# Hyena filter and maxout FFN: the filter's second stage by halves, with one sum moved to GpSimd

## The chip, the cores and the metric

The kernel runs on one core of one Trainium2 chip. The metric is the device time in microseconds (us) of one execution; for the kernel before it is the median of three runs. One further execution was recorded by the hardware profiler, and every line of a profile below is from it. The engines are named as in the profile: PE is TensorE's matmul, PEld its weight load, DVE is VectorE, ACT is ScalarE, POOL is GpSimd, SP is SyncE (which issues DMAs).

## The reference

The first block is a long convolution by FFT, gated by x; the second is a feed-forward block with the maximum of three products. Shapes: x and v are 4 x 12544 x 128, the filter's features 64, the FFN's width 768.

```python
def _attn_ref(x, v, pos_emb, w1, w2) -> np.ndarray:
    B, S, D = x.shape
    h_mlp = np.maximum(pos_emb @ w1, 0.0) @ w2
    pos = np.arange(S, dtype=np.float32)
    window = np.exp(-0.01 * pos)[:, None]
    h_filt = h_mlp * window
    u = x * v
    L = 2 * S
    Uf = np.fft.rfft(u, n=L, axis=1)
    Hf = np.fft.rfft(h_filt, n=L, axis=0)
    y = np.fft.irfft(Uf * Hf[None, :, :], n=L, axis=1)[:, :S, :]
    return (x * y).astype(np.float32)

def _moe_ref(x, w1, w2, w3, w_out) -> np.ndarray:
    h = np.maximum(np.maximum(x @ w1, x @ w2), x @ w3)
    return (h @ w_out).astype(np.float32)
```

## The kernel before

The transforms are matmuls with tables, in two stages each way. A sequence position is split into a block number and a place s2 in the block (0 to 127). The first stage transforms over the block numbers and leaves 90 frequencies, each a complex number (two 64-row halves of 128 partitions) for each place s2. The second stage goes over the places, with one 128 x 256 table per frequency (`wt_const`) that also holds the twiddle factors. The places are kept in two sets of 64 (r = 0 and 1: odd and even places, in reversed order), so a frequency's second stage is two matmuls, one for each r, and the outputs of a frequency and of its partner half a turn on are the sum and the difference of the two.

The prologue loads the weights, computes the filter's small MLP, and leaves two tiles of first-stage spectra: `spec` of u = x * v for batch 0 (128 partitions x 90 frequencies x 2 halves r x 128 channels) and `specH` of the filter's 64 features (128 x 90 x 2 x 64). The filter's second matmul, `w2`, is applied after the transform.

Then comes the first loop, which is where the change lies. It runs over 45 groups g of two neighbouring frequencies (k = 0, 1), one group entering at each step s, with the work of several groups in flight:

- `s_minus(g)` (L1103, POOL) stores the negated r = 0 half of the group's columns of specH in `minus`.
- `s_second(g)` (L1115, PE; L1120, ACT) is the filter's second stage. For each k, r and q it multiplies a 128 x 64 piece of specH by a 128 x 128 table into the upper or lower 64 partitions (q) of one PSUM bank: q = 0 adds both halves r, q = 1 adds the r = 1 half to the negated r = 0 half. ACT copies the 128 x 256 result to `G`.
- `g_second(g)` (L167 through `second` and `halves_mm`; ACT copies the even half to `eo`, L203) is the same stage for the signal, with 8 matmuls, and `g_butterfly(g)` (L197 and L198, DVE) makes its sum and difference, from PSUM and `eo`, in `xt`.
- One step later `g_swap` (L623, L624, ACT) writes `xs`, the real and imaginary halves of xt exchanged, one of them negated; `s_filter` (L1133, PE) applies `w2x` to G, 16 matmuls of 64 x 64 tiles, and ACT copies the 128 x 1024 product to `ht` (L1149).
- Two steps later `s_store` (L1154, POOL) stores ht in `hd`, in DRAM, for the other batches. The pointwise product of signal and filter is `g_re` (L629: xt times the filter's real part), `g_im` (L633: xs times its imaginary part, L634: the sum of both), and `g_unfold` (L641) makes sum and difference of the partners in `ab`.
- Three steps later `g_third` (L167 on `ab`, PE) is the first inverse stage; ACT copies it to `zs` (L656) and SP stores that in `zd`.

Engines run their instructions in the order in which the program issues them; semaphores are set between engines where tiles are handed on. Within a step the order of the calls is: s_second(s), s_minus(s+1), g_second(s), g_swap(s-1), s_filter(s-1), g_third(s-3), s_store(s-2), then for the group s-2 g_re, g_im and g_unfold, then g_butterfly(s). In the later steps the first units of batch 1 are loaded, multiplied (`u_mul`, L386 on DVE, in five steps of the loop) and transposed (`u_turn`, L399 and L402, in four). Steps 45 to 47 drain the loop and mix in more of batch 1.

Buffers that matter: `G`, `xt`, `xs`, `ab` and the filter's PSUM bank have two, `ht` two for even groups and two more (in the `uT` pool) for odd groups below 34; from group 34 on two in all. The PSUM banks of g_second and g_third are a pool of three.

From about 300 us to the end run the fused loops: inverse transform and FFN of batch b interleaved with the convolution of batch b + 1, and a last batch with a seven-product scheme. Nothing of it is changed. Three rows of it serve as measures: L596, L599 and L603 are its product, sum on POOL, and unfold, of the same sizes as L633, L634 and L641.

Of the kernel before, what the change touches and what calls it, by code (L numbers as in the profile page):

```python
# [10 lines left out]
FP32 = mybir.dt.float32  # L11
I32 = mybir.dt.int32
U16 = mybir.dt.uint16
ALU = mybir.AluOpType
ACTF = mybir.ActivationFunctionType
PSUM = bass.MemoryType.PSUM
P = 128
# [78 lines left out]
def kernel(  # L96
# [15 lines left out]
    nc = tc.nc  # L112
    NG, _, _, B, NB = x.shape
    FO, S = posT.shape
    D = w2.shape[1]
    DFF = moe_w1.shape[1]
    NF = DFF // P
    NK = N1 // 2
# [76 lines left out]
    def butterfly(ps, eo, xs):  # L195
        v = ps[:, :].rearrange("p (k r d) -> p k r d", k=2, r=2)
        nc.vector.tensor_tensor(out=xs[:, :, 0, :], in0=eo[:], in1=v[:, :, 0, :], op=ALU.add)  # L197
        nc.vector.tensor_tensor(out=xs[:, :, 1, :], in0=eo[:], in1=v[:, :, 0, :],  # L198
                                op=ALU.subtract)
# [80 lines left out]
    specH = pin.tile([P, N1, 2, FO], FP32, name="specH")  # L280
# [6 lines left out]
    w2x = pin.tile([P, D], FP32, name="w2x")  # L287
# [96 lines left out]
    def u_mul(u, eng=nc.vector):  # L384
        a, v = us[u]
        eng.tensor_tensor(out=a[:], in0=a[:], in1=v[:], op=ALU.mult)  # L386
# [221 lines left out]
    def g_second(g):  # L608
        ps = state["cv"][1].tile([P, 512], FP32, tag="cv", name="ps2")
        second(ps, ws.pop((g, 0)), g)  # L610
        eo = state["cv"][0].tile([P, 2, D], FP32, tag="eo", name="eo", bufs=2)
        evens(ps, eo)
        pss[g], eos[g] = ps, eo

    def g_butterfly(g):
        xt = state["cv"][0].tile([P, 2, 2, D], FP32, tag="x", name="xt", bufs=state["xb"])
        butterfly(pss.pop(g), eos.pop(g), xt)
        xts[g] = xt

    def g_swap(g):  # L620
        xt = xts[g]
        xs = state["cv"][0].tile([P, 2, 2, D], FP32, tag="xs", name="xs", bufs=2)
        nc.scalar.mul(xs[0:64], xt[64:128], -1.0)  # L623
        nc.scalar.copy(xs[64:128], xt[0:64])  # L624
        xss[g] = xs

    def g_re(g):
        xt = xts[g]
        nc.vector.tensor_tensor(out=xt[:], in0=xt[:], in1=hts[g][0][:], op=ALU.mult)  # L629

    def g_im(g, apart=False):
        xt, xs = xts[g], xss.pop(g)
        nc.vector.tensor_tensor(out=xs[:], in0=xs[:], in1=hts.pop(g)[1][:], op=ALU.mult)  # L633
        (nc.gpsimd if apart else nc.vector).tensor_tensor(  # L634
            out=xt[:], in0=xt[:], in1=xs[:], op=ALU.add)
# [9 lines left out]
    def g_third(g):  # L645
        w, ab = ws.pop((g, 1)), abs_.pop(g)
        ps = state["cv"][1].tile([P, 512], FP32, tag="cv", name="ps3")
        for k in range(2):
            for q in range(2):
                halves_mm(ps[:, (2 * k + q) * D:(2 * k + q + 1) * D], w[:, k, q, :],  # L650
                          ab[:, k, q, :], k == 0 and q == 0, True)
        if g < NK - 2:
            zs = state["cv"][0].tile([P, 2, 256], FP32, tag="z", name="zs", bufs=2)
        else:
            zs = lwp.tile([P, 2, 256], FP32, tag="w1", name="zs")
        nc.scalar.copy(zs[:].rearrange("p k f -> p (k f)"), ps[:])  # L656
        nc.sync.dma_start(
            zd[0][2 * g:2 * g + 2].rearrange("k c t f -> (c t) k f"), zs[:])
# [309 lines left out]
    def load_dir(g, a):  # L968
        w = lwp.tile([P, 2, 2, P], FP32, tag=f"w{a}", name="wt")
        nc.sync.dma_start(w[:].rearrange("p k r m -> p (k r m)"), wt_d[g, :, a, :])  # L970
        return w
# [60 lines left out]
    for f in range(0, FO, 4):  # L1032
        quad([hs[:, f + i] for i in range(4)], (f1h[:, 0], f1h[:, 1]), specH[:, :, :, f:f + 4])
        u, k = divmod(f // 4, 4)
# [10 lines left out]
    wf, wi = {}, {}  # L1045
    for u in range(4, NU, 2):
        t = uts.pop(u)
        for v in range(2):
            if u + 4 < NU:
                u_mul(u + 4 + v)  # L1050
            at = 4 * (u + v)
# [17 lines left out]
    for i in (1, 2):  # L1069
        nc.vector.tensor_tensor(out=w_sb[i][:], in0=w_sb[i][:], in1=w_sb[0][:],  # L1070
                                op=ALU.subtract)
# [3 lines left out]
    cvp = pro.enter_context(tc.tile_pool(name="cvp0", bufs=3))  # L1075
# [10 lines left out]
    def bank():  # L1086
        return next(free)

    state = {"cv": (cvp, cps), "xb": 2, "bank": bank, "wide": ("ht", 2),
             "turn": lambda: sps.tile([P, 512], FP32, tag="pl", name="pst")}  # L1090
    Gs, minus = {}, {}

    def fold(f):
        pt = cps.tile([P, 512], FP32, tag="cv", name="pt")
# [2 lines left out]
        nc.scalar.copy(w1t[:, 0], pt[:, 0:D])  # L1097
        return lambda: halves_mm(pl[:, 0:D], w1t[:, 0], wo_sb[:, f, :], f == 0, f == NF - 1)

    def s_minus(g):  # L1100

        m = cvp.tile([P, 2, FO], FP32, tag="minus", name="minus", bufs=1)
        nc.gpsimd.tensor_single_scalar(m[:], specH[:, 2 * g:2 * g + 2, 0], -1.0, op=ALU.mult)  # L1103
        minus[g] = m

    def s_second(g):


        ps = gps.tile([P, 512], FP32, tag="g", name="gps")
        m = minus.pop(g)  # L1110
        for k in range(2):
            for r in range(2):
                for q in range(2):
                    lhsT = m[:, k] if q and r == 0 else specH[:, 2 * g + k, r, :]
                    nc.tensor.matmul(ps[64 * q:64 * q + 64, k * P:(k + 1) * P],  # L1115
                                     lhsT, wf[g][:, k, r, :],
                                     start=(k == 0 and r == 0), stop=True,
                                     skip_group_check=True)
        G = cvp.tile([P, 2, 2, 64], FP32, tag="G", name="G", bufs=2)
        nc.scalar.copy(G[:].rearrange("p k c j -> p (k c j)"), ps[:, 0:2 * P])  # L1120
        Gs[g] = G

    def s_filter(g):


        G = Gs.pop(g)
        ps = sps.tile([P, 1024], FP32, tag="h", name="sps")
        for ri in range(2):
            for k in range(2):
                for q in range(2):  # L1130
                    for h in range(2):
                        at = 512 * q + (2 * ri + k) * D
                        nc.tensor.matmul(  # L1133
                            ps[64 * h:64 * h + 64, at:at + D],
                            G[64 * q:64 * q + 64, k, ri, :], w2x[64 * q:64 * q + 64],
                            start=(ri == 0 and k == 0), stop=True, skip_group_check=True)
        v = ps[:].rearrange("p (q m d) -> p m q d", q=2, d=D)
        if g == NK - 1:
            hts[g] = []
            for c in range(2):  # L1140
                ht = lwp.tile([P, 2, 2, D], FP32, tag="w0", name="ht")
                nc.scalar.copy(ht[:], v[:, 2 * c:2 * c + 2])
                hts[g].append(ht)
            return
        if g % 2 and g < NK - 11:
            ht = utp.tile([P, 2, 2, 2, D], FP32, tag="uT", name="ht")
        else:
            ht = cvp.tile([P, 2, 2, 2, D], FP32, tag="ht", name="ht", bufs=2)
        nc.scalar.copy(ht[:].rearrange("p r k q d -> p (r k) q d"), v)  # L1149
        hts[g] = ht[:, 0], ht[:, 1]  # L1150

    def s_store(g):
        for c in range(2):
            nc.gpsimd.dma_start(  # L1154
                hd[g, 64 * c:64 * c + 64],
                hts[g][c][64 * c:64 * c + 64].rearrange("p k q d -> p (k q d)"))
# [7 lines left out]
    def folding(f):  # L1164
        folded.append(fold(f))
        if len(folded) > 2:
            folded.pop(0)()

    def unit(u):
        u_first(u, (bank(), bank()), "x")  # L1170

    s_minus(0)
    for s in range(NK + 3):
        if s < NK:
            ws[s, 0] = wf[s]
            s_second(s)
            if s + 1 < NK:
                s_minus(s + 1)
            g_second(s)
            wf.pop(s)  # L1180
            if s + 3 < NK:
                wf[s + 3] = load_dir(s + 3, 0)
        if 1 <= s <= NK:
            g_swap(s - 1)
            s_filter(s - 1)
        if s >= 3:
            ws[s - 3, 1] = wi.pop(s - 3)
            g_third(s - 3)
            if s < NK:
                wi[s] = load_dir(s, 1)  # L1190
        ready = [g for g in {NK: (s - 2, s - 1)}.get(s, (s - 2,)) if 0 <= g and s <= NK]
        for g in {NK - 2: (s - 2, s - 1), NK - 1: (s - 1,), NK: (s - 1,)}.get(s, (s - 2,)):
            if 0 <= g and s <= NK:
                s_store(g)
        for g in ready:
            g_re(g)
            g_im(g)
            g_unfold(g)
        if s < NK:
            g_butterfly(s)  # L1200

        if s in muls:
            u_mul(muls[s])
        if s in turns:
            u_turn(turns[s])
        if s in loads:
            u_load(1, loads[s])
        if s == NK:
            unit(0)
            pl = sps.tile([P, 512], FP32, tag="pl", name="pl")  # L1210
        if s == NK + 1:
            for f in range(3):
                folding(f)
# [22 lines left out]
    cvp = conv.enter_context(tc.tile_pool(name="cvp", bufs=3))  # L1236
# [5 lines left out]
    state = {"bank": lambda: next(pairs), "wide": ("cb", 3)}  # L1242
# [67 lines left out]
    state = {"bank": lambda: next(singles)}  # L1310
# [17 lines left out]
    for i in range(0, NT, 2):  # L1328
        h = {}
        X, Y = banks if i % 4 == 0 else banks[::-1]  # L1330
        for j, (name, f) in enumerate(ORDER):
# [6 lines left out]
            if step > 2 and weights:  # L1338
                out, a1, a2 = weights.pop(0)
# [59 lines left out]
```

## Time and profile before

| what | value |
|---|---|
| runs | 2234.57, 2238.08, 2239.85 us; median 2238.08 |
| profiled execution | 2231.93 us, span 2230.1 us, mean granted PE clock 0.999 |
| busy over the span | PE 99%, PEld 58%, DVE 70%, ACT 55%, POOL 52% |
| the first loop | first matmul of s_second at 111.2 us, of the last group at 279.1 us |
| in 180 to 190 us of it | PE 10.00 of 10.00, DVE 9.41, ACT 8.87, POOL 5.08, DMA share 0.89 at 293 GB/s |

The span is cut into rows by line of the program. For a line the profile gives the number of instructions and the duration of one; the rows that the change touches, over the whole loop:

| line | engine, operation | count | us of one (min / median / max) |
|---|---|---|---|
| L1103 | POOL, minus <- specH, 128x128 | 45 | 0.520 / 0.735 / 1.069 |
| L1115 | PE, gps, 64x128 outputs (two records a matmul) | 720 | 0.272 / 0.273 / 0.323 |
| L1120 | ACT, G <- gps, 128x256 | 45 | 0.372 / 0.390 / 0.392 |
| L1149 | ACT, ht <- sps, 128x1024 | 44 | 1.012 / 1.012 / 1.015 |
| L634 | DVE, xt <- xt + xs, 128x512 | 45 | 0.691 / 0.692 / 0.694 |
| L641 | DVE, ab <- xt, 128x256 | 90 | 0.416 / 0.424 / 0.510 |
| L599 (fused loop) | POOL, cb <- cb + xs, 128x512 | 135 | 1.261 / 1.272 / 1.794 |

A PE row's duration is the latency of one pipelined matmul: sixteen records of L1115 start over 0.87 us. Instructions of DVE and ACT that don't depend on each other overlap by up to 0.1 us, so the time that one costs its engine is read from start to start.

### The profile page before, as it was taken

The page shows a single profiled execution, that of the slowest core. Times are in us where ns is not written, and L with a number is a line of the kernel's source. Part 1 is how long each engine was busy: PE and PEld are TensorE (multiplying, and loading weights), DVE is VectorE, ACT ScalarE, POOL GpSimd, SP SyncE. Part 2 cuts the span into 40 slices and gives each one's busy share as a digit, 9 for nine tenths or more (in the row PEclk, how much of TensorE's full clock was granted, in tenths as well). Part 3 has the DMA queues.
Part 4 walks back from the last instruction along what each step waited for, and adds up shares of the span by engine and source line. Part 5 has one row for each costly group of instructions (what it writes and reads, how often), then busy time and mean ns, then how long its engine had stood idle before and what let it go on. Part 6 is the DMA issues. An engine that isn't in the chain of part 4 may idle for free.

```text
span 2230.1 us, 77908 instructions
## 1 busy us (share of the span) xinstructions
PE 2209.7 (99%) x32015; PEld 1301.2 (58%) x32015; DVE 1555.8 (70%) x3245; ACT 1216.9 (55%) x2223; POOL 1164.0 (52%) x1580
## 2 busy tenths in 40 slices
PE   9999989999999999999999999999999999999999
PEld 8999955555555555555555555545555545666665
DVE  5689966668878766677888866668878754545443
ACT  3688955556666555556666655556666622222222
POOL 1145457634545566634554467635454426666665
PEclk9999999999999999999999999999999999999999
DMA  8778989979999999869999999869999732222221
GB/s 197 183 237 278 304 183 199 184 169 236 246 247 235 231 192 180 174 159 248 237 243 237 223 205 177 175 156 240 243 244 237 205 79 58 58 67 71 64 58 24
DMA packets 491335, 411.66 MB, mean 185 GB/s; under 512 B 289406, under 2 KB 407920, under 8 KB 490979
## 3 DMA queue, kind: packets, MB, share of 16 engines
q1 hardware_dynamic: 443689, 274.50, 56.0%
q0 software_dynamic: 45808, 130.25, 21.5%
q8 instruction: 252, 4.13, 0.8%
q10 hardware_dynamic: 1482, 1.93, 0.4%
q14 instruction: 104, 0.85, 0.1%
HBM read 262.85 MB, written 84.67 MB: 156 GB/s over the span
## 4 chain that ended last, share of the span: by engine, by line
PE 87%; DMA 6%; DVE 3%; SPq 2%; issue 1%; POOL 1%; ACT 0%; DVEq 0%; POOLq 0%; ACTq 0%
PE hps L167 40%; PE ops L167 16%; PE ops L899 6%; PE ps L167 4%; PE cps L167 3%; PE cps L449 3%; PE ps L176 3%; DMA ht<-hd 3%; PE cps L547 2%; PE sps L1133 2%; PE cps L557 2%; PE gps L1115 2%; DMA sq<-spec 2%; DMA wt<-wq_const 1%; SPq L520 1%
## 5 line engine op out<-in xcount | busy, mean ns | idle before, releaser
L167 PE MATMUL hps<-gt,w_sb 128*64 128x392 f32 (+1 forms) x7672 | 1154.3, 494 | 1.8 <-DVE hid L838 1.0
L835 ACT ACTIVATE hid<-hps 128x392 f32<-128x392 f32 x768 | 382.7, 498 | 757.3 <-PE hps L167 740.6
L167 PEld LDWEIGHTS hps<-gt,w_sb 128*64 128x64 f32 (+1 forms) x7672 | 423.1, 126 | 445.8 <-issue 410.0
L838 DVE TENSOR_TENSOR hid<-hid,hps 128x392 f32<-128x392 f32 x768 | 428.6, 558 | 346.1 <-PE hps L167 329.6
L167 PE MATMUL ops<-hid,wo_sb 128*64 128x392 f32 x2304 | 476.8, 492 | 0.0
L599 POOL TENSOR_TENSOR cb<-cb,xs 128x512 f32<-128x512 f32 x135 | 177.9, 1318 | 404.0 <-DVE xs L596 379.8
L167 PEld LDWEIGHTS ops<-hid,wo_sb 128*64 128x64 f32 x2304 | 165.6, 137 | 213.6 <-issue 213.6
L572 DVE TENSOR_TENSOR cb<-cps,eo 128x512 f32<-128x512 f32 (+1 forms) x288 | 175.2, 650 | 72.5 <-ACT eo L569 71.4
L853 POOL DMA_DIRECT2D out_dram<-ot x96 | 76.6, 798 | 232.4 <-ACT ot L851 216.9
L587 ACT ACTIVATE xs<-cb 32x512 f32<-32x512 f32 x270 | 169.5, 628 | 21.1 <-DVE cb L572 12.3
L588 ACT COPY xs<-cb 32x512 f32<-32x512 f32 x270 | 166.3, 616 | 3.2
L603 DVE TENSOR_TENSOR xs<-cb 128x256 f32<-128x256 f32 x270 | 149.0, 599 | 6.2 <-POOL cb L599 6.2
L429 ACT COPY uT<-turned 113x512 uint16<-113x512 uint16 x180 | 125.9, 770 | 0.1
L386 POOL TENSOR_TENSOR ut<-ut 128x392 f32<-128x392 f32 x90 | 93.3, 1037 | 40.7 <-DMA ut<-in_vr_dram 36.0
L167 PEld LDWEIGHTS cps<-f4p,even 90*64 90x64 f32 x1552 | 87.2, 138 | 35.9 <-issue 33.2
L768 POOL DMA_DIRECT2D xT<-in_x_dram x172 | 101.5, 604 | 3.5 <-DVE hid L838 2.5
L471 DVE TENSOR_TENSOR low<-high,cps 128x180 f32<-128x180 f32 x186 | 54.7, 335 | 68.7 <-ACT high L461 68.7
L580 POOL DMA_DIRECT2D zd<-cb x135 | 95.4, 706 | 13.7 <-DVE cb L572 10.9
L924 POOL DMA_DIRECT2D out_dram<-o x120 | 72.7, 612 | 47.1 <-DVE o L917 45.6
L167 PE MATMUL cps<-f4p,zt 90*64 90x49 f32 x1552 | 95.9, 222 | 0.1
L1103 POOL TENSOR_SCALAR minus<-specH 128x128 f32<-128x128 f32 x45 | 34.4, 764 | 117.7 <-PE gps L1115 93.0
L413 POOL COPY planes<-ut 128x392 uint16<-128x392 uint16 x180 | 95.7, 566 | 0.0
(165 smaller groups left out, 3483.5 us busy)
## 6 DMA issues: line engine op xcount, KB each, us to landing
ht<-hd SPq DMA_DIRECT2D x264, 256.0 KB, 7.4
wt<-wq_const POOLq DMA_DIRECT2D x144, 256.0 KB, 5.2
zd<-cb POOLq DMA_DIRECT2D x135, 256.0 KB, 6.5
zt<-zd SPq DMA_DIRECT2D x384, 90.0 KB, 3.7
sq<-spec SPq DMA_DIRECT2D x528, 64.0 KB, 5.7
ut<-in_xr_dram SPq DMA_DIRECT2D x128, 196.0 KB, 4.1
ut<-in_vr_dram SPq DMA_DIRECT2D x128, 196.0 KB, 4.3
wt<-wt_const SPq DMA_DIRECT2D x90, 256.0 KB, 4.8
```

The lines of the kernel that those rows point to most:

```text
L167: nc.tensor.matmul(out[h:h + w], lhsT[:, h:h + w], rhs, start=start, stop=stop, skip_group_check=True)
L413: nc.gpsimd.tensor_copy(w[:, h, :, :, 0:HB], a[:].bitcast(U16).rearrange("p s (m e h) -> p h s e m", e=2, h=2)[:, h])
L429: nc.scalar.copy(uts[u][0:HR, 8 * (u % 2):8 * (u % 2) + 8].rearrange("n s r t -> n (s r t)").bitcast(U16).rearrange("n (s r t h) -> n h s ...
L572: nc.vector.tensor_tensor(out=cb[:, a, lo:hi], in0=ps[:, lo:hi], in1=eo[:, lo:hi], op=op)
L587: nc.scalar.mul(xs[at:at + 32], xt[at + 32:at + 64], -1.0)
L588: nc.scalar.copy(xs[at + 32:at + 64], xt[at:at + 32])
L599: nc.gpsimd.tensor_tensor(out=xts[g], in0=xts[g], in1=xs[:], op=ALU.add)
L603: nc.vector.tensor_tensor(out=ab[:, q], in0=y[:, 0], in1=y[:, 1], op=(ALU.subtract, ALU.add)[q])
L768: eng.dma_start(xT[c * NG:(c + 1) * NG].rearrange("d i p n -> d (i p) n"), x[:, 4 * i:4 * i + 8, c, b, :])
L835: nc.scalar.activation(h[:], pa[:, 0:N], Relu)
L838: nc.vector.tensor_tensor(out=h[:], in0=h[:], in1=pb[:, 0:N], op=ALU.max)
L899: nc.tensor.matmul(ps[32 * q:32 * q + 32, 0:H2], w[:, m:m + 32], rhs[:, H2 * c:H2 * c + H2], start=start, stop=True, skip_group_check=True)
```

## The change

Three things are changed, all in the first loop.

The filter's second stage multiplies each half r once: 4 matmuls for 8, the r = 0 products in one 128 columns of the bank and the r = 1 products in the next, the frequency k in the upper or lower 64 partitions. ACT copies the r = 0 products to `low` (128 x 128), and a new function `s_sums` on DVE makes r1 + r0 and r1 - r0 in G. `s_minus` and its tile are gone. G now has k on its partitions and q in its columns, and the loops and views of s_filter are turned around to match; number and size of its matmuls and copies stay.

The sum of the pointwise product (`g_im`'s second instruction) is made by POOL in steps 2 to 43, by the argument `apart`, which the function had already.

The unfolding comes last in a step, behind s_sums and g_butterfly. With that, three groups' xt are alive at once: every third group's is put into the first four frequencies of specH, which steps 0 and 1 have read by then.

```diff
     def g_butterfly(g):
-        xt = state["cv"][0].tile([P, 2, 2, D], FP32, tag="x", name="xt", bufs=state["xb"])
+        if g % 3 == 2:
+            xt = specH[:, 0:4].rearrange("p k r f -> p (k r f)").rearrange(
+                "p (k r d) -> p k r d", k=2, r=2)
+        else:
+            xt = state["cv"][0].tile([P, 2, 2, D], FP32, tag="x", name="xt", bufs=state["xb"])
         butterfly(pss.pop(g), eos.pop(g), xt)
...
-    def s_minus(g):
-
-        m = cvp.tile([P, 2, FO], FP32, tag="minus", name="minus", bufs=1)
-        nc.gpsimd.tensor_single_scalar(m[:], specH[:, 2 * g:2 * g + 2, 0], -1.0, op=ALU.mult)
-        minus[g] = m
-
     def s_second(g):
         ps = gps.tile([P, 512], FP32, tag="g", name="gps")
-        m = minus.pop(g)
-        for k in range(2):
-            for r in range(2):
-                for q in range(2):
-                    lhsT = m[:, k] if q and r == 0 else specH[:, 2 * g + k, r, :]
-                    nc.tensor.matmul(ps[64 * q:64 * q + 64, k * P:(k + 1) * P],
-                                     lhsT, wf[g][:, k, r, :],
-                                     start=(k == 0 and r == 0), stop=True,
-                                     skip_group_check=True)
+        for r in range(2):
+            for k in range(2):
+                nc.tensor.matmul(ps[64 * k:64 * k + 64, r * P:(r + 1) * P],
+                                 specH[:, 2 * g + k, r, :], wf[g][:, k, r, :],
+                                 start=(r == 0), stop=True, skip_group_check=True)
+        low = cvp.tile([P, P], FP32, tag="low", name="low", bufs=1)
+        nc.scalar.copy(low[:], ps[:, 0:P])
+        lows[g] = low, ps
+
+    def s_sums(g):
+        low, ps = lows.pop(g)
         G = cvp.tile([P, 2, 2, 64], FP32, tag="G", name="G", bufs=2)
-        nc.scalar.copy(G[:].rearrange("p k c j -> p (k c j)"), ps[:, 0:2 * P])
+        for q, op in enumerate((ALU.add, ALU.subtract)):
+            nc.vector.tensor_tensor(out=G[:, q].rearrange("p c j -> p (c j)"),
+                                    in0=ps[:, P:2 * P], in1=low[:], op=op)
         Gs[g] = G
...
         for ri in range(2):
-            for k in range(2):
-                for q in range(2):
+            for q in range(2):
+                for k in range(2):
                     for h in range(2):
-                        at = 512 * q + (2 * ri + k) * D
+                        at = 512 * k + (2 * ri + q) * D
                         nc.tensor.matmul(
                             ps[64 * h:64 * h + 64, at:at + D],
-                            G[64 * q:64 * q + 64, k, ri, :], w2x[64 * q:64 * q + 64],
-                            start=(ri == 0 and k == 0), stop=True, skip_group_check=True)
-        v = ps[:].rearrange("p (q m d) -> p m q d", q=2, d=D)
+                            G[64 * k:64 * k + 64, q, ri, :], w2x[64 * k:64 * k + 64],
+                            start=(ri == 0 and q == 0), stop=True, skip_group_check=True)
+        v = ps[:].rearrange("p (k r m) -> p r k m", k=2, r=2)
...
-        nc.scalar.copy(ht[:].rearrange("p r k q d -> p (r k) q d"), v)
+        nc.scalar.copy(ht[:].rearrange("p r k q d -> p r k (q d)"), v)
...
-    s_minus(0)
     for s in range(NK + 3):
         if s < NK:
             ws[s, 0] = wf[s]
             s_second(s)
-            if s + 1 < NK:
-                s_minus(s + 1)
             g_second(s)
...
         for g in ready:
             g_re(g)
-            g_im(g)
+            g_im(g, 1 < s < NK - 1)
+        if s < NK:
+            s_sums(s)
+            g_butterfly(s)
+        for g in ready:
             g_unfold(g)
-        if s < NK:
-            g_butterfly(s)
```

More of the change, by code (lines that the diff above doesn't have):

```diff
@@ L1090 @@
              "turn": lambda: sps.tile([P, 512], FP32, tag="pl", name="pst")}
-    Gs, minus = {}, {}
+    Gs, lows = {}, {}
     def fold(f):
@@ L1141, in s_filter @@
                 ht = lwp.tile([P, 2, 2, D], FP32, tag="w0", name="ht")
-                nc.scalar.copy(ht[:], v[:, 2 * c:2 * c + 2])
+                nc.scalar.copy(ht[:].rearrange("p k q d -> p k (q d)"), v[:, c])
                 hts[g].append(ht)
```

## The prediction

> **What bounds the kernel now.** I read the page first: TensorE (PE) is busy 99% of a 2230.1 us span, so a change counts only where it shortens PE's stream or lets PE wait. The change touches the first loop alone, which by the start of its first matmul (111.2 us) and of its last group's (279.1 us) is 168 us long. So the second view is the chain of work in order of time, cut to that loop. Its columns are start, length, and what.
>
> ```profile
> 101.31 2.63 PE ps L176 x64
> ...
> 184.41 0.87 PE gps L1115 x16
> 185.29 0.87 PE ps L167 x16
> 186.16 1.03 PE sps L1133 x32
> 187.19 1.02 PE ps L167 x16
> 188.22 0.87 PE gps L1115 x16
> ```
>
> One step of the loop is 188.22 - 184.41 = 3.81 us, and all of it is PE: the filter's second stage (gps), g_second (ps), s_filter (sps), g_third (ps), with no other engine between them. The loop is bound by PE. The question is then how much room the other engines leave below 3.81 us. The third view is the timeline of VectorE (DVE) over one step; columns are start, length, instruction, count.
>
> ```profile
> 184.80 0.42 DVE L198 TENSOR_TENSOR xt<-eo,ps 128x256 f32<-128x256 f32 x1
> 185.18 0.69 DVE L629 TENSOR_TENSOR xt<-xt,ht 128x512 f32<-128x512 f32 x1
> 185.79 0.78 DVE L633 TENSOR_TENSOR xs<-xs,ht 128x512 f32<-128x512 f32 x1
> 186.60 0.69 DVE L634 TENSOR_TENSOR xt<-xt,xs 128x512 f32<-128x512 f32 x1
> 187.40 0.76 DVE L641 TENSOR_TENSOR ab<-xt 128x256 f32<-128x256 f32 x2
> 188.26 0.42 DVE L197 TENSOR_TENSOR xt<-eo,ps 128x256 f32<-128x256 f32 x1
> ```
>
> DVE has nearly no room: from L197 at 184.46 to L197 at 188.26 it is never idle for more than 0.1 us. The same view for ScalarE (ACT):
>
> ```profile
> 185.04 0.59 ACT L656 COPY zs<-ps 128x512 f32<-128x512 f32 x1
> 185.52 0.39 ACT L1120 COPY G<-gps 128x256 f32<-128x256 f32 x1
> 186.26 0.37 ACT L203 COPY eo<-ps 128x256 f32<-128x256 f32 x1 [0.35 <-PE ps L167]
> ```
>
> ACT waits 0.35 us a step for PE and works the remaining 3.46. So three engines lie within a tenth of each other, and cutting PE alone moves the bound to the next one.
>
> **The change part by part.**
>
> *PE, 0.44 us a step removed.* s_second goes from 8 matmuls to 4 of the same shape, 0.87 -> 0.436 us. The four now stream different data through the two column halves where the eight shared it. Bounds: 0 saved if such halves don't overlap (4 x 0.218 us), 0.436 if they do. The L176 line decides: there the halves also stream different tables, and 64 records of 90 columns take 2.63 us, 41 ns each, against 0.87 / 16 = 54 ns for 128 columns here (90/128 of it is 38). They overlap; I take 0.436. PE's own step becomes 3.37 us.
>
> *ACT.* The copy of G (128x256, 0.39) becomes a copy of low (128x128); the row of L1097 has that shape from PSUM at 0.266 us. ACT's work is 3.46 - 0.12 = 3.34 us. The eviction of the product (L1149, 1.01) keeps its 1024 elements, and the s_filter matmuls their number, tiles and rotation; only the order of columns differs: no cost taken.
>
> *GpSimd (POOL), the negation goes.* L1103 (45 x, mean 764 ns) kept no other engine waiting; its end costs nothing, and gives DVE a little: L633 takes 0.78 us beside it and 0.69 without it (280.60 us).
>
> *DVE.* L634 leaves for steps 2 to 43 (42 of them). Two sums of 128x128, PSUM and SBUF in, come. No row has the shape: from L471 (128x180, 0.334) and L197 (128x256, 0.422), both PSUM and SBUF, the line through them gives 0.27 us each, 0.20 to 0.27 from start to start; bounds 0.40 and 0.67 for the two. DVE's busy work falls; by work alone it would fit 3.37.
>
> *The new wait.* L634's add now runs on POOL, between im's product (L633) and unfold (L641), and unfold is moved behind the sums and the butterfly. The same trio exists later in the kernel, in the timelines of DVE and POOL at 470 us: product L596, POOL's add L599 of the same 128x512, unfold L603.
>
> ```profile
> 470.41 0.69 DVE L596 TENSOR_TENSOR xs<-xs,ht 128x512 f32<-128x512 f32 x1
> ...
> 472.55 0.76 DVE L603 TENSOR_TENSOR xs<-cb 128x256 f32<-128x256 f32 x2 [0.50 <-POOL cb L599]
> 473.23 0.56 DVE L838 TENSOR_TENSOR hid<-hid,hps 128x392 f32<-128x392 f32 x1
> ```
>
> ```profile
> 471.25 1.27 POOL L599 TENSOR_TENSOR cb<-cb,xs 128x512 f32<-128x512 f32 x1 [3.78 <-DVE xs L596]
> ```
>
> From the product's end (471.10) to the unfold's start (472.55) are 1.45 to 1.47 us: 0.15 to 0.18 to POOL, 1.27, 0.03 back. The cover that DVE has for it is the two sums (0.42) and the butterfly (0.34 + 0.42 by L197 and L198), together 1.18. So DVE stands still some 0.29 us in every step, and behind the unfold in its queue stand the next group's L629 and L633, the sums and the butterfly; PE's s_filter waits for the sums and g_third for the unfold. The cycle of DVE and POOL is then: L629 to L633 0.61 (185.18 to 185.79), L633 0.69, over and back 0.17 + 1.27 + 0.03, unfold 0.76, and from its end to the next L629 between -0.08 (L603 to L838 above) and +0.10 (L641 to L197), of which I take +0.02: 3.55 us, 3.45 to 3.63 with the ends and the scatter of L599 (0.02). That is above PE's 3.37 and ACT's 3.34, so it sets the step.
>
> The GPSIMD Engine Reference of the Trainium skill, section 4.1, speaks against this move: it says that two-input elementwise work is about twice as slow on GpSimd and sends it to VectorE. The trace agrees nearly: 1.27 against 0.69, 1.84 times. With the page's factor the add would be an estimated 1.38 us, and the gain below 6 us where I have 11.
>
> What lies beside the add matters. L599 is 1.26 to 1.28 us where DVE's neighbours (L838, L825) read one operand from PSUM, but at 497.48 us it took 1.77 with four unfolds beside it, whose two operands are both in SBUF, and the slowest L603 took 1497 ns against a median of 415. In the new order the instructions beside the add are the sums and the butterfly, each with a PSUM operand, and the unfold waits: I take 1.27.
>
> The same reference, section 8, names the rule: GpSimd contends with VectorE instructions that have two SBUF inputs. These rows agree, and by it sums and butterfly are spared.
>
> *POOL's queue.* Per step it issues two stores of hd (0.55 each, L1154) and then the add: 1.1 + 1.27 of 3.55. The stores need only ht, as L629 does, and take 1.1 us where L629 and L633 take 1.3: they are done before the add is due. But a store now stands behind the add of the step before. In the last ten groups ht has two buffers, and its next writer (L1149) waits for the store's landing: add, 1.1 issue, a landing of 4.4 (median, up to 7.3), L1149 1.0, then L629 to the add (about 2.7 with the add) is 10.5 us for three steps, 3.5 each. At the median that hides behind 3.55; a few long landings may cost 1 or 2 us in all.
>
> *The rest.* The third xt buffer, in columns of specH already read, adds no instruction. DMA moves the same bytes: 46.76 MB in the loop's 176 us (266 GB/s), 284 GB/s in 11 us less, against 346 in the busiest 10 us of now; weight loads land in at most 6.3 us and are asked three steps ahead.
>
> *The sum.* Follow L629 from group 0 to group 43, whose tail is a DVE chain of unchanged length until the spectra's last sums (L485) at 292 us. Before: 118.37 to 283.80. After: group 0's L629 comes 2 x 0.436 earlier (two shorter s_second precede it), 117.50; 42 cycles of c; five u_mul on DVE at 0.47 (274.92 to 275.39); step 44, with the add on DVE again, about 4.0 (products and add 2.03, sums 0.42, butterfly 0.75, unfold 0.80). That is 123.85 + 42c, a gain of 159.95 - 42c: with c = 3.55, **10.9 us**. With 3.45 it is 15.1, with 3.63 7.5. The tail and the fused loops behind it are the same instructions, PE bound: the gain passes on whole. The profiled execution took 2231.93 us (span 2230.1), 6.15 below the median of the runs, 2238.08; from its time the sum gives 2221, from the median **2227**.
>
> **The rivals.**
> 1. *PE stays the bound*: the wait for POOL is covered better than I count (c near 3.37). For it: DVE's spacing can shrink (-0.08). Against: the 1.45 of 470 us is measured whole and 1.18 of cover is not enough. At most 45 x 0.436 = 19.6 us: 2218.5 to 2222.
> 2. *Part of it given back in the last third*: hd landings hold L1149 and the uT copies (2 x 0.58 in four steps) hold ACT. For: landings up to 7.3 us. Against: ACT waited 0.3 us for hd in all. Gain 2 to 7: about 2233.
> 3. *The halves don't overlap*: s_second keeps 0.87 us, PE its 3.81, and 3.55 hides behind it: no change, 2238. Against: the L176 line.
> 4. *Slower: the add on POOL is stretched by DVE beside it* (L634's add, sums and butterfly reading low and eo from SBUF meanwhile). Each 0.1 us on it is 4.2 us in all; the gain is gone at c = 3.81, an add of 1.53. At the 1.77 seen at 497 us, c is 4.05 and the kernel loses 10: 2248. Against: that neighbour had two SBUF operands.
>
> **How the numbers follow.** Forecast 0.60 (2223 to 2231), rival 1 0.10, rival 2 0.12, rival 3 0.06, rival 4 0.12. About 0.2%, 4.5 us, is what a measurement can tell from no change here. Faster: 0.60 + 0.10 + four fifths of rival 2 = 0.79; same: the rest of it and rival 3, 0.09; slower 0.12. The likeliest gives 2227; the range from rival 1 to the far end of rival 2 is 2219 to 2237, with the runs' own spread (2234.57 to 2239.85) in it.
>
> **What would show it.** Right: the loop's step 3.5 to 3.6 us; unfold idle about 0.3 us a step, released by POOL; PE waiting 0.15 to 0.2 us a step for DVE; gps at 0.44; the add at 1.27; ACT's wait moved from PE to others. Wrong: a step of 3.4 with PE unbroken (rival 1), gps at 0.87 (3), the add above 1.5 (4), L1149 waiting for hd (2). What would overturn the sum is a wait of DVE that I count as covered, the sums for low or the butterfly for eo.

## The result and the profile after

| | before | after |
|---|---|---|
| median of 7 runs | 2234.77 us (2233.15 to 2239.85) | 2226.94 us (2221.21 to 2230.29) |
| span of the profiled execution | 2230.1 us | 2219.4 us |
| first loop, one step (L629 before, L633 after; mean over groups 17 to 29) | 3.805 us | 3.401 us |
| the same instruction, group 0 to group 43 | 165.4 us | 153.9 us |
| first product gt of the fused loops | 303.76 us | 290.63 us |
| from there to the end of the span | 1926.3 us | 1928.7 us |

The changed kernel is faster: ratio 0.9954, 95% interval 0.9939 to 0.9970, or 7 to 14 us; the medians differ by 7.8 us. In the profiled executions the loop gives 13.1 us (that of the changed kernel, 2221.21 us, is the fastest of its seven); what follows the loop runs the same instructions.

In the changed kernel's lines most numbers have moved: L1110 is the second stage (L1115 before), L1114 the copy to low, L1121 the sums, L633, L637 and L638 the product and its add (L629, L633, L634), L645 the unfold (L641), L1151 ht (L1149), L1156 the stores (L1154).

One step in the timeline of the changed kernel, the rows of DVE, POOL and PE alone; columns are start, length, engine, line, instruction, count, and in brackets the engine's idle time and who ended it:

```profile
182.83 0.61 PE L1110 MATMUL gps<-wt,specH 128*64 128x128 f32 x8
183.19 0.48 DVE L1121 TENSOR_TENSOR G<-gps,low 128x128 f32<-128x128 f32 x2
183.27 1.04 PE L167 MATMUL ps<-spec,wt 128*64 128x128 f32 x16
183.43 1.27 POOL L638 TENSOR_TENSOR xt<-xt,xs 128x512 f32<-128x512 f32 x1 [1.12 <-DVE xs L637]
183.59 0.41 DVE L197 TENSOR_TENSOR xt<-eo,ps 128x256 f32<-128x256 f32 x1
183.92 0.41 DVE L198 TENSOR_TENSOR xt<-eo,ps 128x256 f32<-128x256 f32 x1
...
184.73 0.76 DVE L645 TENSOR_TENSOR ab<-xt 128x256 f32<-128x256 f32 x2 [0.40 <-POOL xt L638]
...
185.41 0.68 DVE L633 TENSOR_TENSOR specH<-specH,ht 128x512 f32<-128x512 f32 x1
186.01 0.68 DVE L637 TENSOR_TENSOR xs<-xs,ht 128x512 f32<-128x512 f32 x1
186.25 0.61 PE L1110 MATMUL gps<-wt,specH 128*64 128x128 f32 x8
```

The second stage now has 183.27 - 182.83 = 0.44 us of PE before the next group of matmuls starts. POOL's add is 1.27 us long, the sums and the butterfly run beside it, and the unfold starts 0.03 us after it, having waited 0.40. From one L1110 to the next are 3.42 us. The chain of work shows what sets them (start, length, what):

```profile
202.54 0.46 issue
203.00 0.69 DVE xs L637
203.84 1.27 POOL xt L638
205.11 1.03 POOL hd L1156 x2
206.14 1.00 issue
207.19 1.28 POOL specH L638
208.50 0.76 DVE ab L645 x2
```

Before, this chain was PE from end to end; now it goes round product, add and unfold, and PE is not in it. (Where it shows the stores of hd instead, it has stayed on POOL's queue between two adds.)

At the loop's end stands something else, in the timeline of step 43:

```profile
260.38 0.68 DVE L637 TENSOR_TENSOR xs<-xs,ht 128x512 f32<-128x512 f32 x1
...
263.16 1.01 ACT L1151 COPY ht<-sps 128x1024 f32<-128x1024 f32 x1
...
264.46 1.04 POOL L1156 DMA_DIRECT2D hd<-ht  x2 [3.36 <-ACT ht L1151]
...
265.52 1.27 POOL L638 TENSOR_TENSOR specH<-specH,xs 128x512 f32<-128x512 f32 x1
...
266.83 0.76 DVE L645 TENSOR_TENSOR ab<-specH 128x256 f32<-128x256 f32 x2 [4.08 <-POOL specH L638]
...
267.31 1.97 PE L167 MATMUL ps<-ab,wt 128*64 128x128 f32 x16 [1.99 <-DVE ab L645]
```

The product of group 41 is ready at 261.06, but POOL adds it only at 265.52. In step 43 the program stores two groups, 41 and 42, ahead of the add, and group 42's ht is done at 264.17 (263.16 + 1.01). POOL stands in its queue for that, DVE 4.08 us behind POOL, and PE 1.99 us behind DVE. And PE's next 16 records take 1.97 us where they took 1.15. The windows of the changed kernel show why (stretch, its length, then PE, PEld, DVE, ACT, POOL busy with counts, the granted PE clock, DMA share, GB/s):

```profile
265.00:268.00 3.00, 1.01 (x18) 0.73 (x12) 1.17 (x3) 1.26 (x3) 1.78 (x2) 0.82 0.79 190
268.00:271.00 3.00, 2.42 (x35) 2.04 (x36) 2.96 (x9) 2.01 (x4) 1.07 (x2) 0.50 0.43 117
271.00:274.00 3.00, 3.00 (x44) 2.34 (x43) 2.96 (x6) 2.14 (x5) 1.04 (x2) 0.54 0.80 232
```

The granted clock falls to 0.50 at the end of the gap; by the three means it stays there for some 7 us. The kernel before had such a stretch only later, at 291 us.

### The profile page after: what moved, and what is told of

It reads as the page before. It is cut to its first block, busy times and chain, and to the rows that moved or that the text cites. A ratio compares the mean times of both kernels' runs of the same rounds, so it can differ in the third digit from the quotient of the medians.

```text
span 2219.4 us, 77166 instructions
## 1 busy us (share of the span) xinstructions
PE 2194.1 (99%) x31655; PEld 1297.3 (58%) x31655; DVE 1534.6 (69%) x3293; ACT 1210.9 (55%) x2223; POOL 1179.0 (53%) x1577
## 3 DMA queue, kind: packets, MB, share of 16 engines
q8 instruction: 249, 4.08, 0.8%
## 4 chain that ended last, share of the span: by engine, by line
PE 84%; DMA 6%; DVE 3%; POOL 3%; issue 2%; SPq 1%; ACT 1%; POOLq 0%; DVEq 0%; ACTq 0%
PE hps L167 42%; PE ops L167 17%; PE ops L903 6%; PE cps L167 3%; PE cps L449 3%; PE ps L176 3%; PE cps L547 3%; PE cps L557 2%; DMA sq<-spec 2%; DMA ht<-hd 2%; DMA zt<-zd 1%; PE ps L167 1%; DMA wt<-wq_const 1%; POOL xt L638 1%; PE last L167 1%
## 5 line engine op out<-in xcount | busy, mean ns | idle before, releaser
L167 PEld LDWEIGHTS hps<-gt,w_sb 128*64 128x64 f32 (+1 forms) x7672 | 430.6, 126 | 439.1 <-issue 407.9
L587 ACT ACTIVATE xs<-cb 32x512 f32<-32x512 f32 x270 | 169.4, 628 | 21.5 <-DVE cb L572 12.6
L603 DVE TENSOR_TENSOR xs<-cb 128x256 f32<-128x256 f32 x270 | 148.7, 598 | 6.5 <-POOL cb L599 6.5
L580 POOL DMA_DIRECT2D zd<-cb x135 | 95.0, 704 | 14.6 <-DVE cb L572 10.7
L547 PE MATMUL cps<-sq,wt 64*64 64x128 f32 x2160 | 90.6, 276 | 4.6 <-DMA wt<-wq_const 2.9
```

Of the source, the lines that this page charges most:

```text
L167: nc.tensor.matmul(out[h:h + w], lhsT[:, h:h + w], rhs, start=start, stop=stop, skip_group_check=True)
L547: nc.tensor.matmul(ps[64 * a:64 * a + 64, at:at + D], w[64 * r:64 * r + 64, k, a, :], t[64 * r:64 * r + 64, k, :, a], start=(k == 0), stop ...
L587: nc.scalar.mul(xs[at:at + 32], xt[at + 32:at + 64], -1.0)
L603: nc.vector.tensor_tensor(out=ab[:, q], in0=y[:, 0], in1=y[:, 1], op=(ALU.subtract, ALU.add)[q])
```

## The experiments

Ten kernels, each the changed kernel with an edit. The loop is read from the profile, since there it repeats: the step over groups 17 to 29 agreed within 0.005 us and the stretch from group 0 to group 30 within 0.2 us in the six profiles whose edits leave them alone, whereas the six or seven runs of one of these kernels spread over 6 to 9 us.

| kernel | step, us | group 0 to 43, us | gt at, us | median or single run, us |
|---|---|---|---|---|
| before | 3.805 | 165.4 | 303.76 | 2234.77 |
| after | 3.401 | 153.9 | 290.63 | 2226.94 |
| e1, last add on DVE | 3.402 | 150.5 | 288.10 | 2224.93 (ratio to before 0.9948, 0.9928 to 0.9967) |
| e2, all adds on DVE | 3.657 | 160.0 | 296.88 | 2231.61 (one) |
| e3, unfold before the sums | 4.456 | 195.3 | 333.86 | 2265.73 (one) |
| e4, second stage twice | 3.855 | 170.6 | 307.14 | 2237.10 (one) |
| e5, add in two | 3.591 | 160.6 | 297.75 | 2229.82 (one) |
| e6, half the add | 3.381 | 153.2 | 290.05 | 2229.01 (one) |
| e7, e1 and ht in specH | 3.404 | 151.1 | 288.66 | 2220.54 (0.9928, 0.9908 to 0.9948) |
| e8, e1 and u_mul before the unfold | 3.400 | 149.6 | 286.95 | 2223.70 (one) |
| e9, all three | 3.404 | 150.7 | 288.30 | 2223.18 (0.9940, 0.9926 to 0.9955) |
| e10, the same kernel as e8 | 3.405 | 150.0 | 287.49 | 2221.77 (0.9934, 0.9921 to 0.9948) |

### e2: all adds on DVE

```diff
-            g_im(g, 1 < s < NK - 1)
+            g_im(g)
```

> The second stage by halves and the unfold last, but no add on POOL. Theory (the cycle of DVE and POOL sets the step of 3.40 us): DVE alone then needs 0.60 + 0.72 + 0.62 for the product and the add, 0.40 for the sums, 0.66 for the butterfly, 0.70 for the unfold, 3.70 in all, so the step is 3.70, the gain over before only 0.1 us a step; gt at about 290.6 + 42 x 0.30 - 3.3 = 300 us. Rival (PE sets the step, POOL's share is not needed): 3.40 stays, gt at 288 to 291.

The step is 3.657, near the theory's 3.70. The timeline of DVE in this kernel shows it without a pause (busy for 59.41 of 60 us in 150 to 210, against 53.13 in the changed kernel), each product, add and sum starting as soon as the one before lets it:

```profile
181.91 0.69 DVE L633 TENSOR_TENSOR xt<-xt,ht 128x512 f32<-128x512 f32 x1
182.52 0.68 DVE L637 TENSOR_TENSOR xs<-xs,ht 128x512 f32<-128x512 f32 x1
183.24 0.69 DVE L638 TENSOR_TENSOR xt<-xt,xs 128x512 f32<-128x512 f32 x1
183.84 0.48 DVE L1121 TENSOR_TENSOR G<-gps,low 128x128 f32<-128x128 f32 x2
```

So the halved matmuls, with their sums on DVE, could use only 0.15 of their 0.44 us before DVE binds; moving the add gives 0.26 more.

### e3: unfold before the sums

```diff
+        for g in ready:
+            g_unfold(g)
         if s < NK:
             s_sums(s)
             g_butterfly(s)
-        for g in ready:
-            g_unfold(g)
```

> The unfold goes back ahead of sums and butterfly, the add stays on POOL. Theory: nothing covers POOL's 1.47 us any more, the cycle grows by the 1.06 us of sums and butterfly from 3.40 to about 4.46 us, some 43 us over the loop: slower than before the change by 30 us. Rival (PE sets the step and the add is hidden with room to spare): the step grows by less than 0.4 us.

4.456 us, as the theory had it: the same instructions on the same engines, and the order alone is worth 1.05 us a step. In this form the change would have been slower than before by some 30 us (gt at 333.86 against 303.76). The timeline of DVE in this kernel shows the wait, now 1.39 us:

```profile
180.04 0.68 DVE L637 TENSOR_TENSOR xs<-xs,ht 128x512 f32<-128x512 f32 x1
182.11 0.76 DVE L645 TENSOR_TENSOR ab<-specH 128x256 f32<-128x256 f32 x2 [1.39 <-POOL specH L638]
182.79 0.48 DVE L1121 TENSOR_TENSOR G<-gps,low 128x128 f32<-128x128 f32 x2
```

### e5 and e6: the add in two instructions, and half of it

```diff
-        (nc.gpsimd if apart else nc.vector).tensor_tensor(
-            out=xt[:], in0=xt[:], in1=xs[:], op=ALU.add)
+        if apart:
+            for k in range(2):
+                nc.gpsimd.tensor_tensor(out=xt[:, k], in0=xt[:, k], in1=xs[:, k], op=ALU.add)
+            return
+        nc.vector.tensor_tensor(out=xt[:], in0=xt[:], in1=xs[:], op=ALU.add)
```

e6 makes only the one for k = 0 and leaves out the other half of the sum.

> POOL's add is made in two instructions of 128x256. The line through L599 (512 columns, 1.27 us) and L386 (392, 1.025 us) leaves 0.23 us for a column count of zero, so two halves take about 1.50 us. Theory (the cycle of DVE and POOL sets the step): the step grows by the same 0.23, from 3.40 to 3.63 us, 9 to 10 us in the loop. Rival (PE sets the step): PE's 3.37 covers it, less than 0.1 us a step.

> In steps 2 to 43 POOL adds the first frequency of each group only; the second one's sum is left out. Theory: POOL's add takes about 0.75 us, less than DVE's cover of 1.06 us, so the unfold no longer waits for POOL and the next bound shows: PE at 3.37 us, or DVE's own stream, 3.40 less the 0.33 to 0.41 that it waits now, whichever is longer. Step 3.37 to 3.38, with PE not waiting for DVE. Rival (DVE's own stream sets the step, not its wait): 3.40 stays and PE goes on waiting.

The two halves of e5 took 1.41 us together (0.72 each, some of it overlapped), 0.14 more than the one, and the mean step grew by 0.19, to 3.591. One of its steps, with a late hand-over to POOL, took 3.85 us; all the others took 3.56 to 3.58, which is the changed kernel's 3.42 and the 0.14 (its shorter steps of 3.36 do not occur here). The theory's mechanism holds; its 0.23 was too much, since the second instruction's start lies under the end of the first. In e6 the step fell to 3.381 (3.368 over groups 5 to 27), and DVE no longer waits for POOL. The list of waits in 140 to 210 us of e6 (total, times, longest) has for DVE only

```profile
DVE xt L633 <- ACT ht L1153: 5.1, 14, 0.6
```

and its like for specH. The chain of work in e6 is PE from end to end again:

```profile
184.36 0.44 PE gps L1112 x8
184.79 0.87 PE ps L167 x16
185.67 1.03 PE sps L1137 x32
186.70 1.02 PE ps L167 x16
187.73 0.44 PE gps L1112 x8
```

PE, at the 3.37 that the prediction counted, is the next bound. (The share of busy time could not tell: PE counts as busy for 60.00 of 60 us in 150 to 210 both here and in the changed kernel.) POOL's add costs 0.02 to 0.03 us a step over that, no more. All of e6's head start (100.0 us to group 30, against 102.1) was lost in the last third, 42.3 us from group 30 to 41 against 40.4, where its waits name DMA: 2.5 us of DVE for u_mul's input, 1.6 of ACT for zd, 0.5 of PE for tables.

### e4: the second stage twice

```diff
-                nc.tensor.matmul(ps[64 * k:64 * k + 64, r * P:(r + 1) * P],
-                                 specH[:, 2 * g + k, r, :], wf[g][:, k, r, :],
-                                 start=(r == 0), stop=True, skip_group_check=True)
+                for c in range(2):
+                    nc.tensor.matmul(
+                        ps[64 * k:64 * k + 64, (2 * c + r) * P:(2 * c + r + 1) * P],
+                        specH[:, 2 * g + k, r, :], wf[g][:, k, r, :],
+                        start=(r == 0 and c == 0), stop=True, skip_group_check=True)
```

> The four matmuls of the filter's second stage are issued twice, the second time into unused columns of the same bank: PE has the eight matmuls of before, everything else is as changed. Theory: PE's own step is 3.37 us and the cycle of DVE and POOL is 3.40, so PE gets the bound back at 3.81 us a step, 0.41 more, some 17 us in the loop: the time of the kernel before within 3 us. Rival (PE has much room and the gain came from DVE's relief): the step stays below 3.6.

PE has the bound back, at 3.855. The chain of e4 reads as that of the kernel before, but for one number:

```profile
183.19 0.92 PE gps L1111 x16
184.11 0.87 PE ps L167 x16
184.99 1.03 PE sps L1137 x32
186.02 1.02 PE ps L167 x16
```

0.92 where eight matmuls took 0.87. Here each pair in a row goes to the same column half; before, the halves took turns. That this costs the 0.05 is likely but wasn't tried by itself. All the rest of the change brings nothing without the halved matmuls: gt at 307.14 against 303.76; the stall of step 43 (8.04 us from group 41 to 42) and 42 times 0.05 more than account for that.

### e1: the last add on DVE

```diff
-            g_im(g, 1 < s < NK - 1)
+            g_im(g, 1 < s < NK - 2)
```

> Theory: in step 43 the stores of groups 41 and 42 stand ahead of group 41's add in POOL's queue, so the add waits for group 42's ht and the unfold stands still for 4.1 us. With that one add back on DVE, the time from L633 of group 41 to that of group 42 falls from 7.74 us to about 4.4 (group 42's ht is ready at 264.2, the step's start at 259.8), and everything behind comes 3.3 us earlier: the fused loop's first product (gt) from 290.6 to about 287.3 us. Rival: ht itself is late (the landing of hd or ACT's uT copies hold it); then the wait only moves and 1 us or less is gained.

From group 41 to 42 are 4.43 us instead of 7.74, the 3.3 us of the theory. The timeline of e1, DVE in step 43, shows the queue gone and ht as what is left:

```profile
260.53 0.69 DVE L638 TENSOR_TENSOR specH<-specH,xs 128x512 f32<-128x512 f32 x1
...
262.20 0.75 DVE L645 TENSOR_TENSOR ab<-specH 128x256 f32<-128x256 f32 x2
263.64 0.69 DVE L633 TENSOR_TENSOR xt<-xt,ht 128x512 f32<-128x512 f32 x1 [0.69 <-ACT ht L1151]
```

gt came 2.5 us earlier, not 3.3: 1.3 of it went in the stretch behind group 43 (20.8 us against 19.5), and 0.5 came from an earlier start.

### e7, e8, e9, e10: towards a better version

e7 is e1 with ht of groups 34 to 43 in specH:

```diff
-        if g % 2 and g < NK - 11:
-            ht = utp.tile([P, 2, 2, 2, D], FP32, tag="uT", name="ht")
-        else:
-            ht = cvp.tile([P, 2, 2, 2, D], FP32, tag="ht", name="ht", bufs=2)
+        if g < NK - 11:
+            ht = (utp.tile([P, 2, 2, 2, D], FP32, tag="uT", name="ht") if g % 2 else
+                  cvp.tile([P, 2, 2, 2, D], FP32, tag="ht", name="ht", bufs=2))
+        else:
+            at = 4 + 8 * (g % 5)
+            ht = specH[:, at:at + 8].rearrange("p k r f -> p (k r f)").rearrange(
+                "p (r k q d) -> p r k q d", r=2, k=2, q=2)
```

e8 and e10 are e1 with

```diff
+        if s in muls and s < NK:
+            u_mul(muls[s])
         for g in ready:
             g_unfold(g)
-        if s in muls:
+        if s in muls and s == NK:
             u_mul(muls[s])
```

and e9 has both.

> The kernel with the last add on DVE, and ht of groups 34 to 43 in five places of specH that have been read, in place of two buffers. Theory: L1151 waits for the landing of hd 1.1 us in all; that goes, and with it up to 1.1 us of the loop against the kernel with the last add on DVE, if ACT is on the path there. Rival: the landing (5.6 us in the chain of waits) is what holds the last third; then 2 us or more.

Neither: L1154 (ht in e7) no longer waits for hd, but from group 30 to 41 e7 took 41.3 us, 1.0 more than e1. The timeline of e7 shows other DMAs in its place:

```profile
229.42 0.66 PE L1110 MATMUL gps<-wt,specH 128*64 128x128 f32 x8 [1.80 <-DMA wt<-wt_const]
...
230.06 0.59 ACT L660 COPY zs<-ps 128x512 f32<-128x512 f32 x1 [1.84 <-DMA zd<-zs]
```

The late table did not lengthen the product's step, 3.82 us there as in e1 (3.84). The next one took 5.22 us for 3.90, and in the list of waits in 212 to 262 us stands what held DVE in it, u_mul's input:

```profile
DVE ut L386 <- DMA ut<-in_vr_dram: 1.2, 1, 1.2
```

In this execution the tables landed a median of 5.6 us after their issue and up to 7.6, against 5.0 and 6.3 in the changed kernel and 4.7 and 6.3 in the kernel before. The last third is where loads for the next batch join in (379 GB/s in 220 to 230 us of the changed kernel). u_mul waited for its input for 1.4 us in e9 too, which also has ht in specH, and for 0.4 and 0.3 in e8 and e10, which haven't; whether the places of ht have to do with it was not tried. So the 1 us in the buffers of ht is neither won nor refuted.

> The kernel with the last add on DVE, and u_mul (128x392, two SBUF operands) in five steps put before the unfold, into the 0.33 to 0.41 us in which DVE waits for POOL's add. Theory: beside the add a DVE instruction with two SBUF operands is held (L603 took up to 1497 ns for 415), so u_mul lasts until the add ends or close to it and the step of u_mul stays at 3.8 to 3.9 us or longer. Rival (no contention): u_mul of 0.56 us hides for 0.4 us, and these steps fall to 3.5 us, 2 us in all.

In between. The five steps with u_mul took 3.67 to 3.88 us instead of 3.84 to 3.97 in the changed kernel. DVE and POOL in the timeline of e8:

```profile
227.80 1.27 POOL L638 TENSOR_TENSOR specH<-specH,xs 128x512 f32<-128x512 f32 x1 [1.06 <-DVE xs L637]
...
228.69 0.81 DVE L386 TENSOR_TENSOR ut<-ut 128x392 f32<-128x392 f32 x1
...
229.42 0.75 DVE L645 TENSOR_TENSOR ab<-specH 128x256 f32<-128x256 f32 x2
```

u_mul is 0.81 to 0.88 us long beside the add and 0.57 clear of it, so some 0.25 to 0.3 of the 0.4 us of idle time is lost to this stretching. What is left is 0.17 us in four of the five steps, 0.7 in all (in the fifth, u_mul waited 0.39 us for its load).

> The last add on DVE, ht of groups 34 to 43 in specH, and u_mul before the unfold, together. If the three gains are independent: the fused loop's first product (gt) comes 3.3 us earlier by the first (measured 2.5), about 1 by u_mul (measured 1.1) and up to 1 by ht, so at 286 to 287 us against 290.6 of the changed kernel; step of the middle stretch 3.40 as before. Rival: in the last third the DMA is the limit (a table's load landed 7.5 us after its issue and held PE for 1.8 us in the kernel with ht in specH), then ht's places bring nothing or less than nothing, gt at 287 to 289.

> The same without ht in specH: the last add on DVE and u_mul before the unfold, now timed. gt at 287 us as in its first look (286.95); in time some 3.5 us below the changed kernel, 0.15%, which the spread of the runs will hardly show; against the kernel before about 0.993.

e10 repeats e8 in the loop (150.0 us from group 0 to 43, against 149.6). e9 adds nothing to it (150.7; u_mul waited 1.4 us for its input, 0.5 went to late tables), which is its rival's answer. By the loop the best version is e10: 3.8 us less than the changed kernel from group 0 to 43, 3.1 to gt; its ratio to the kernel before, 0.9934, is the 0.993 expected. In the whole time the intervals of after, e1, e7, e9 and e10 overlap, so their order is not shown by the runs; the loop's own times are.

## Why the prediction was right, and where it was not

**The bound.** Right as put, but by little: not PE at 3.37 but the cycle of DVE and POOL. e3, e5 and e2 show that the order, the add's length and its engine each move the step by about what the cycle says; e6 shows PE at 3.37 to 3.38 right below. The rival that PE stays the bound missed by 0.03 us: the two bounds lie that close, which the prediction, with 0.18 between them, did not see. By the signs that it named, a step of 3.4 us with PE unbroken spoke for rival 1, and the step is 3.40 with PE counted busy throughout. What decides against the rival is the chain, without PE, and e5, whose steps grew by what the add grew.

**The length of the cycle.** Mis-sized, 3.55 for 3.40, and below the low end of 3.45. The terms as measured: L633 to L637 0.60 (0.61 taken), L637 0.68 (0.69), to POOL 0.16, and 0.09 where xt lies in specH (0.17 taken), add 1.27, back 0.03, unfold 0.76, and from its end to the next L633 -0.08 (+0.02). Two groups in three take 3.42, the third 3.36. The term that failed is the last: the low end, from L603 to L838, was the right row, and the row before the change (+0.10, from unfold to butterfly) was not, for there the next instruction had a wait of its own: with two buffers of xt, the butterfly writes the one that the unfold has just read. (The prediction's sentence on an add of 1.38 us has a slip: its sum then gives a gain of 6.2 us, not below 6. The add took 1.27.)

**The cover.** The sums took 0.48 us (0.28 each) and 0.40 from start to start, the butterfly 0.33 a piece, as taken; the unfold waited 0.33 to 0.41 us where 0.29 was counted.

**PE and ACT.** The second stage fell to 0.44; halves that stream different data do overlap. low took 0.28 (0.27 taken). PE's wait for DVE was foretold as 0.15 to 0.2 us a step and is 0.03, the step's 3.40 less PE's 3.37. The list of waits does show PE's weight loads 0.17 us behind the unfold, 3.1 us in 18 steps between 140 and 210 us; but e6, where PE sets the step, has the same pause behind the sums (3.4 us, 20 times), and the kernel before has it without a releaser (2.9 us, 17 times), so it is no cost of the cycle.

**POOL's queue.** Right for the common step: the stores never delayed the add. What the prediction missed is step 43, where the program stores two groups ahead of the add. The prediction named the store behind the add as a danger and not the second store in front of it. It cost 7.74 us instead of the 3.55 counted, and e1 shows the cause.

**The last third.** hd landings held L1151 for 1.1 us in all, within the 1 or 2 us named. That loads are "asked three steps ahead" was too kind: landings grew from 4.7 to 5.0 us (median), and PE waited for tables, 0.5 us in e6 and 1.8 in e7, once the step was at 3.4.

**The sum.** By its own stretches: group 0 to 30, 106.5 predicted and 102.1 measured; 30 to 41, 41.4 and 40.4; 41 to 42, 3.55 and 7.74; 42 to 43, 4.0 and 3.66. In all 155.5 against 153.9, so the 10.9 us came out as 12.6 at group 43, 13.1 at gt and 10.7 in the span. That the total is so near is the meeting of two errors, a cycle too long by 0.15 us in 41 groups (6 us) and a stall of 4.2 us that wasn't seen. That the time fits to 0.1 us is luck besides: 2227 was 10.9 us below a median of three runs, 2238.08; over seven runs that median is 2234.77, and the difference of the medians 7.8.

## What to carry to other kernels

When three engines lie within a tenth of each other, a cut on the first is worth only what the second leaves: price the cycle that goes through two engines, wait and hand-over included, from a place where the same trio already runs. An instruction moved to another engine is paid in waiting unless independent work stands between its issue and its use; here that order was worth 1.05 us a step, more than the whole cut. Read the first and last steps of a loop for extra instructions in the queue of the engine to which the work is moved: one store too early cost 3.3 us of a gain of 13.

## What the runs showed of the hardware

The instructions behind the first gt are the same in all twelve profiles, and took from 1926.3 to 1937.1 us; at the two ends the mean granted PE clock of the execution was 0.999 and 0.995. These eleven microseconds are as much as the change itself, so medians of six or seven runs order these versions poorly, and the loop's own times order them better. What makes the difference was not tried.

In the changed kernel PE lost its full clock with a gap of 1.99 us (0.50 in 268 to 271 us above). The Trainium skill, TensorE: Matmul & The Clock Gate, "Why this matters for your kernels", asks only that there be no idle gaps beyond about 3 us; the measurement here is stricter. It is no fixed bound either: a gap of 1.85 or 1.86 us at the loop's end was followed by a mean clock of 0.50 in e1 (274 to 277 us) and 0.56 in e10 (271 to 274), and by the full clock, 1.00 from 268 to 283 us, in e8 and e9.

POOL's add beside DVE instructions with one operand in PSUM kept its 1.26 to 1.29 us in all 42 steps and left them at their lengths, while u_mul, with both operands in SBUF, was stretched from 0.57 to 0.81 and 0.88 us. That is the contention that the GPSIMD Engine Reference of the skill (section 8) states, here with its price on DVE's side and none on POOL's, whose add stayed at 1.27 us beside u_mul too.
